# Second product of a fused attention and feed-forward kernel: tokens stationary, or w_out stationary in 64-row tiles

## The chip, the cores and the metric

The kernel runs on one core of a Trainium2 chip. The metric is the device time of one execution in microseconds (us): lower is better. Besides the times there is a profile of one execution, which lists every instruction of the engines with its start and length.

The engines that matter are TensorE (PE: matrix products; its weight loads are listed as PEld), VectorE (DVE: elementwise work, 32x32 block transposes), ScalarE (ACT: activation functions, copies and casts) and SyncE (SP), whose queue issues all DMA transfers of this kernel. SBUF is the on-chip memory of 128 partitions; PSUM holds what TensorE sums, in 8 banks of 128 partitions x 512 fp32 numbers.

## The reference

Two stages in float32 over 32768 tokens of 192 features. The first is a dynamic convolution over 7 tokens with softmax weights of 8 heads; the second a feed-forward network with a squared ReLU.

```python
w = exp(weight_gen - max(weight_gen, -1)); w = w / (sum(w, -1) + 1e-9)
out = einsum('bshk,bskhg->bshg', w, x_unf)   # x_unf: the token and the 6 before it
h = out @ w_in            # 192 -> 2048
r = maximum(h, 0)
g = r * r
y = g @ w_out             # 2048 -> 192
```

The weights of the second stage come in as float64 and are decoded on the chip.

## The kernel before

**Tiles and precision.** 64 chunks of 512 tokens (four tiles of 128) are worked through in order. To keep fp32 precision at the speed of TensorE's reduced format (`F32R`), each operand is split into a high part, a cast to that format (ACT), and a low part, the rest (a subtraction on DVE); a product is the sum of high x high, low x high and high x low.

**First product, `mm1(c, j)`.** It makes two of the 16 feature blocks (128 of the 2048 hidden features x 512 tokens), `fb = 2j` and `2j + 1`. The 192 input features are three pieces of 64 (`k` = 0, 1, 2), so the matmuls contract over 64 rows, and the two blocks use the upper and the lower 64 rows of the array side by side. The order of the 9 pairs is: `xh` pieces 0, 1, 2; `xl` pieces 0, 1, 2; `xh` pieces again with the low weights: 18 matmuls of 512 columns. The results lie in a ring of 4 PSUM banks `ph`.

**Between the products.** For each block ACT takes the ReLU out of PSUM into `rg`, squares it in place and casts it to `gh` (`high`; in every chunk from the third the cast of 6 of the 16 blocks is on DVE instead), and DVE makes `gl = rg - gh` (`low`).

**Second product, `mm2(c, fb)`.** A tile of 128 tokens of `gh` or `gl` is stationary (128 x 128), and the weights stream past it: 384 columns (high and low `w_out`) for `gh`, 192 for `gl`, so four pairs of matmuls for each block, summed over 16 blocks in four PSUM banks `acc0` to `acc3` (one per token tile, one buffer each). The sums lie with tokens on partitions. `finish` copies each bank out with ACT, `store` adds the two halves on DVE and writes 512 tokens to memory. Chunk 0 and half of the blocks of chunk 1 use plain fp32 matmuls.

**Attention.** `conv_steps(c, 0)` gives 20 steps for a chunk: 6 of softmax, 13 multiplications and additions of 128 x 768 on DVE, and a turn: a DVE block transpose to `xr`, four transfers to DRAM (`xd`) and two back (`xT`), so that features lie on partitions. Three `split` steps, one for each piece `k`, then make `xh` (a cast on ACT) and `xl` (a subtraction on DVE), which `mm1` of that chunk reads. Since this turn leaves the tokens in another order, `relu` restores it with a permuted write in all chunks from the third.

**Order.** The schedule is written out by hand (`tc.manual_schedule()`): each engine runs its instructions in program order. A chunk has 32 slots: in the first 16 `mm1` stands in every second slot, in the last 16 `mm2(c, 0)` to `mm2(c, 15)` follow one another; `plan` and `plan_conv` hang everything else on slots. The three splits for the next chunk are on slots 27 to 29 of 32.

Of the kernel before, what the change touches and what calls it, by code (L numbers as in the profile page):

```python
# [19 lines left out]
def kernel(  # L20
# [9 lines left out]
    nc = tc.nc  # L30
    B, S, D = x.shape
# [3 lines left out]
    P = 128  # L35
    Q = 32
# [3 lines left out]
    TC = 4  # L40
    NCH = n_chunks or R // TC
    TG = 8
    CPG = TG // TC
    NF = FF // P
    D1 = 64
    ND = D // D1
    N = TC * P
    NJ = NF // 2
    NU = NJ // 2
    WI = ND * P  # L50
    WC = WI + 2 * D
    NSLOT = 2 * NF
    N_PE = 2
    DVE_CAST = 6
    SQ_EARLY = 7
    X_SLOT = 27
    CONV_BEG = 14
    CONV_END = 12

    const = ctx.enter_context(tc.tile_pool(name="const", bufs=1))  # L60
    stage = ctx.enter_context(tc.tile_pool(name="stage", bufs=3))
    xin = ctx.enter_context(tc.tile_pool(name="xin", bufs=2))
    att = ctx.enter_context(tc.tile_pool(name="att", bufs=1))
    xtp = ctx.enter_context(tc.tile_pool(name="xtp", bufs=1))
    gp = ctx.enter_context(tc.tile_pool(name="gp", bufs=8))
    op = ctx.enter_context(tc.tile_pool(name="op", bufs=1))
    dram = ctx.enter_context(tc.tile_pool(name="dram", bufs=2, space=bass.MemoryType.DRAM))
    ps_h = ctx.enter_context(tc.tile_pool(name="ps_h", bufs=4, space=bass.MemoryType.PSUM))
# [7 lines left out]

    ident = const.tile([P, P], F32, name="ident")
    warm = const.tile([P, 1], F32, name="warm")
    W = const.tile([P, 2, NJ, WC], F32R, name="W")

    ctx.enter_context(tc.manual_schedule())

# [51 lines left out]
    def decode_steps(u):  # L134
        raw = raws.pop(u)
        lo, hi = raw[:, :, :, 0], raw[:, :, :, 1]
        w = stage.tile([P, 2, WI], U32, name="du", bufs=4)
        wf = w.bitcast(F32)
        wfull[u] = wf
        j, c0 = 2 * (u % NU), WI * (u // NU)  # L140
        wh, wl = (W[:, q, j:j + 2, c0:c0 + WI] for q in range(2))
        ts, stt = nc.vector.tensor_scalar, nc.vector.scalar_tensor_tensor
        return [
            lambda: nc.scalar.activation(wf, hi.bitcast(F32), AF.Abs),  # L144
            lambda: ts(out=wf, in0=wf, scalar1=MAG_MIN, scalar2=MAG_MAX, op0=ALU.max, op1=ALU.min),
            lambda: ts(out=w, in0=w, scalar1=3, scalar2=0x3FFFFFFF, op0=ALU.logical_shift_left, op1=ALU.bitwise_and),
            lambda: stt(out=w, in0=hi, scalar=0xC0000000, in1=w, op0=ALU.bitwise_and, op1=ALU.bitwise_or),  # L147
            lambda: stt(out=w, in0=lo, scalar=29, in1=w, op0=ALU.logical_shift_right, op1=ALU.bitwise_or),  # L148
            lambda: nc.scalar.copy(wh, wf),  # L149
            lambda: nc.vector.tensor_tensor(out=wl, in0=wf, in1=wh.bitcast(F32), op=ALU.subtract),  # L150
        ]

    decs = {}
# [129 lines left out]

    def relu(c, fb):
        ph = phs.pop((c, fb))
        r = rgs[c, fb] = gp.tile([P, N], F32, name="rg", bufs=NF)
        if c >= N_PE:
            nc.scalar.activation(  # L288
                r.rearrange("p (t q j) -> p t q j", q=P // Q, j=Q),
                ph.rearrange("p (q t j) -> p t q j", q=P // Q, j=Q),  # L290
                AF.Relu,
            )
        else:
            nc.scalar.activation(r, ph, AF.Relu)  # L294

    def square(c, fb):
        r = rgs[c, fb]
        nc.scalar.activation(r, r, AF.Square)  # L298

    def high(c, fb, on_dve):  # L300
        gh = ghs[c, fb] = gp.tile([P, N], F32R, name="gh")
        (nc.vector.tensor_copy if on_dve else nc.scalar.copy)(gh, rgs[c, fb])  # L302

    def low(c, fb):
        gl = gls[c, fb] = gp.tile([P, N], F32R, name="gl")
        nc.vector.tensor_tensor(out=gl, in0=rgs.pop((c, fb)), in1=ghs[c, fb].bitcast(F32), op=ALU.subtract)  # L306

    def in_fp32(c, fb):
        return c == 0 or c == 1 and 1 <= fb <= NF // 2

    def mm2_tile(c, fb, t):
        acc = accs[c][t]
        j, i = divmod(fb, 2)
        sl = slice(WI + i * D, WI + (i + 1) * D)
        ts_ = slice(t * P, (t + 1) * P)
        first, last = fb == 0, fb == NF - 1
        if in_fp32(c, fb):
            nc.tensor.matmul(acc[:, 0:D], rgs[c, fb][:, ts_], wfull[NU + j // 2][:, j % 2, i * D:(i + 1) * D], start=first, stop=last)  # L318
            return
        wo = W[:, :, j, sl]  # L320
        two = [
            (acc[:, 0:2 * D].rearrange("p (q d) -> p q d", q=2), ghs[c, fb][:, ts_], wo),
            (acc[:, 0:D], gls[c, fb][:, ts_], wo[:, 0, :]),
        ]
        if last:
            two.reverse()
        for n, (o, l, rr) in enumerate(two):
            nc.tensor.matmul(o, l, rr, start=(first and n == 0), stop=(last and n == 1))  # L328

    def mm2(c, fb):  # L330
        if fb == 0:
            accs[c] = [ps_o.tile([P, 512], F32, name=f"acc{t}") for t in range(TC)]
        for t in range(TC):
            mm2_tile(c, fb, t)
        if in_fp32(c, fb):
            del rgs[c, fb]
        else:
            del ghs[c, fb], gls[c, fb]

    outs = {}  # L340
# [86 lines left out]
    slots = {}

    def at(c, s, f):
        slots.setdefault((c + s // NSLOT, s % NSLOT), []).append(f)  # L430

    def spread(fs, c, s0, s1):
        for i, f in enumerate(fs):
            at(c, s0 + (s1 - s0) * i // len(fs), f)

    def plan(c):
        for fb in range(NF):
            at(c, fb - fb % 2, lambda fb=fb: relu(c, fb))
        for t in range(TC):
            at(c, 4 * t + 1, lambda t=t: finish(c - 1, t))  # L440
        at(c, 4 * TC - 2, lambda: store(c - 1, 0, TC))
        for fb in range(NF):
            early = fb < SQ_EARLY
            at(c, 2 * fb + 2 if early else NF + fb - SQ_EARLY, lambda fb=fb: square(c, fb))
            if in_fp32(c, fb):
                continue
            on_dve = fb < DVE_CAST and c > 1
            s = 2 * fb + 3 if on_dve else NF + fb - DVE_CAST
            at(c, s, lambda fb=fb, d=on_dve: high(c, fb, d))
            at(c, s, lambda fb=fb: low(c, fb))  # L450

    def plan_conv(m):
        a, b = conv_steps(m, 0) if m > 2 else (conv2[6:], split2)
        if m > 3:
            spread(a, m - 2, CONV_BEG, NSLOT + CONV_END)
        elif m == 3:
            spread(a, 1, NF + 2, NSLOT + CONV_END)
        else:
            spread(a, 1, 0, NF)
        for k, f in enumerate(b):  # L460
            at(m - 1, X_SLOT + k, f)

    for c in range(1, NCH):
        if c == 1:
            plan_conv(2)
            for u, k in ((2, NF + 2), (3, NF + 4), (1, NF + 7)):
                at(1, k, lambda u=u: dec(NU + u, 6))
        plan(c)
        for s in range(NSLOT):
            if s == 2 and c % 2 and (c + 3) // 2 * CPG < NCH:  # L470
                load_group((c + 3) // 2)
            if s == CONV_BEG - 1 and c + 2 < NCH:
                plan_conv(c + 2)
            if s < NF and s % 2 == 0:
                mm1(c, s // 2)
            if s >= NF and not (c == NCH - 1 and s >= NSLOT - 4):
                mm2(c, s - NF)
            for f in slots.pop((c, s), []):
# [38 lines left out]
```

## Time and profile before

| What | Value |
|---|---|
| Time, median of 3 runs | 2278.14 us (2277.9 to 2278.43) |
| Time of the profiled execution | 2278.05 us |
| Span of the profile (first to last instruction) | 2276.3 us |
| DVE busy | 1903.1 us (84%) |
| ACT busy | 1705.7 us (75%) |
| Granted TensorE clock | 1.000 |
| DMA bytes, mean rate | 158.86 MB, 70 GB/s |

The span is what the profile can explain; 1.75 us of the profiled execution lie outside it. A busy time counts the time in which an engine has at least one instruction under way; matmuls overlap, so PE's own busy time says little about its pace, and the distance between starts is the better measure. In rows of the timeline the columns are start, length, engine, line, operation, `out<-in`, shapes, count of merged instructions, and in brackets the idle time before with what ended it.

### The profile page before, as it was taken

How to read it: one execution, taken by the hardware profiler on the slowest of the kernel's cores; microseconds unless marked ns; L12 is line 12 of the kernel's file. 1: busy time of each engine (PE TensorE's matmuls, PEld its weight loads, DVE VectorE, ACT ScalarE, POOL GpSimd, SP SyncE). 2: the span in 40 equal slices, each digit the busy share in tenths (PEclk: the TensorE clock that was granted, in tenths of full speed). 3: DMA queues.
4: the chain of work that ended last, by engine and by line, in shares of the span. 5: the costliest groups of instructions: out<-in, count | busy, mean ns of one | idle time of the engine just before them, and what ended most of it. 6: DMA issues, size and time to landing. Idle time of an engine off the chain costs nothing.

```text
span 2276.3 us, 45075 instructions
## 1 busy us (share of the span) xinstructions
PE 2259.1 (99%) x17648; PEld 2070.4 (91%) x17648; DVE 1903.1 (84%) x2944; ACT 1705.7 (75%) x3206; POOL 1.7 (0%) x7
## 2 busy tenths in 40 slices
PE   7999999999999999999999999999999999999999
PEld 6898999999989999999899999998998999989988
DVE  8888888888888888888888888888888888888884
ACT  5587787787877877878778778777787787777877
POOL 0000000000000000000000000000000000000000
PEclk9999999999999999999999999999999999999999
DMA  6132221322212312213223133131231221322211
GB/s 168 57 85 64 78 82 32 85 78 64 85 36 78 85 57 85 53 61 85 64 78 84 30 84 85 57 85 36 77 85 59 83 60 54 85 69 73 56 33 39
DMA packets 102134, 158.86 MB, mean 70 GB/s; under 512 B 8488, under 2 KB 65704, under 8 KB 97952
## 3 DMA queue, kind: packets, MB, share of 16 engines
q1 hardware_dynamic: 101920, 155.97, 24.5%
q8 instruction: 138, 2.26, 0.4%
q14 instruction: 76, 0.62, 0.1%
HBM read 106.39 MB, written 49.55 MB: 69 GB/s over the span
## 4 chain that ended last, share of the span: by engine, by line
PE 98%; DVE 1%; DMA 0%; ACT 0%; issue 0%; SPq 0%; DVEq 0%; ACTq 0%
PE acc L328 51%; PE ph L280 46%; PE acc L318 1%; DMA xt<-in_x_dram 0%; PE ph L237 0%; DVE pr L195 0%; DVE pr L200 0%; ACT rg L294 0%; DMA raw<-in_moe_w_in_dram 0%; ACT rg L298 0%; ACT du L144 0%; ACT W L149 0%; DVE du L147 0%; DVE du L148 0%; DVE W L150 0%
## 5 line engine op out<-in xcount | busy, mean ns | idle before, releaser
L328 PE MATMUL acc<-W,gh 128*128 128x384 f32 x4000 | 1153.6, 361 | 0.0
L328 PE MATMUL acc<-W,gl 128*128 128x192 f32 x4000 | 992.1, 251 | 0.0
L288 ACT ACTIVATE rg<-ph 128x512 f32<-128x512 f32 x992 | 539.9, 597 | 507.6 <-PE ph L280 495.5
L306 DVE TENSOR_TENSOR gl<-rg,gh 128x512 fp32r<-128x512 f32 x1000 | 691.0, 691 | 201.3 <-ACT gh L302 158.8
L280 PE MATMUL ph<-xh,W 64*128 64x512 f32 x6144 | 802.0, 389 | 3.1 <-ACT W L149 1.7
L328 PEld LDWEIGHTS acc<-W,gh 128*128 128x128 f32 x4000 | 750.8, 188 | 22.2 <-DVE gl L306 21.2
L328 PEld LDWEIGHTS acc<-W,gl 128*128 128x128 f32 x4000 | 762.7, 191 | 0.0
L280 PEld LDWEIGHTS ph<-xh,W 64*128 64x128 f32 x6144 | 588.1, 184 | 115.9 <-issue 11.6
L298 ACT ACTIVATE rg<-rg 128x512 f32<-128x512 f32 x1024 | 644.4, 631 | 0.0
L280 PE MATMUL ph<-xl,W 64*128 64x512 f32 x3072 | 435.3, 387 | 0.0
L195 DVE TENSOR_TENSOR pr<-xt,wt 128x768 f32<-128x768 f32 x448 | 425.7, 951 | 1.4 <-DMA xt<-in_x_dram 1.4
L302 ACT CAST gh<-rg 128x512 fp32r<-128x512 f32 x628 | 389.1, 620 | 18.0
L200 DVE TENSOR_TENSOR pr<-pr 128x768 f32<-128x768 f32 x381 | 362.4, 951 | 0.4
L280 PEld LDWEIGHTS ph<-xl,W 64*128 64x128 f32 x3072 | 296.7, 184 | 52.8 <-DVE xl L220 0.4
L302 DVE CAST gh<-rg 128x512 fp32r<-128x512 f32 x372 | 155.5, 418 | 149.6 <-ACT rg L298 145.5
L351 ACT COPY raw<-acc 128x384 f32<-128x384 f32 x252 | 121.6, 483 | 4.1 <-PE acc L328 4.1
L220 DVE TENSOR_TENSOR xl<-xT,xh 128x512 fp32r<-128x512 f32 x186 | 122.2, 684 | 0.0
L219 ACT CAST xh<-xT 128x512 fp32r<-128x512 f32 x186 | 102.7, 616 | 0.5 <-DMA xT<-xd 0.5
L357 DVE TENSOR_TENSOR o_sb<-raw 128x768 f32<-128x768 f32 (+1 forms) x64 | 60.1, 939 | 4.7 <-ACT raw L351 4.7
L254 DVE STREAM_TRANSPOSE xr<-pr 128x768 f32<-128x768 f32 x62 | 60.2, 971 | 0.0
L181 ACT ACTIVATE wt<-wt 128x224 f32<-128x224 f32 x64 | 24.0, 376 | 13.7 <-DVE wt L180 13.7
L318 PE MATMUL acc<-du,rg 128*128 128x192 f32 x192 | 31.7, 327 | 0.0
(30 smaller groups left out, 269.3 us busy)
## 6 DMA issues: line engine op xcount, KB each, us to landing
xT<-xd SPq DMA_DIRECT2D x124, 384.0 KB, 5.1
xt<-in_x_dram SPq DMA_DIRECT2D x31, 1344.0 KB, 8.7
out_dram<-o_sb SPq DMA_DIRECT2D x63, 384.0 KB, 5.6
xd<-xr SPq DMA_DIRECT2D x248, 96.0 KB, 2.0
wt<-in_weight_gen_dram SPq DMA_DIRECT2D x31, 224.0 KB, 5.5
raw<-in_moe_w_in_dram SPq DMA_DIRECT2D x16, 192.0 KB, 4.0
raw<-in_moe_w_out_dram SPq DMA_DIRECT2D x4, 768.0 KB, 4.6
xt<-in_x_dram SPq DMA_DIRECT2D x2, 384.0 KB, 4.3
```

The costliest lines, as they stand in the source:

```text
L195: tt(out=dst, in0=src, in1=wk.broadcast_to([P, n, G]), op=ALU.mult)
L200: tt(out=prs[k0], in0=prs[k0], in1=prs.pop(k), op=ALU.add)
L219: nc.scalar.copy(xh, src[k])
L220: tt(out=xl, in0=src[k], in1=xh.bitcast(F32), op=ALU.subtract)
L254: nc.vector.transpose(xr.rearrange("p b (t j) -> p t b j", j=Q), prs.pop(0).rearrange("p t (b i) -> p t b i", i=Q),)
L280: nc.tensor.matmul(two[i], w, xx[rows, k], start=(n == 0), stop=(n == len(seq) - 1))
L288: nc.scalar.activation(r.rearrange("p (t q j) -> p t q j", q=P // Q, j=Q), ph.rearrange("p (q t j) -> p t q j", q=P // Q, j=Q), AF.Relu,)
L298: nc.scalar.activation(r, r, AF.Square)
L302: (nc.vector.tensor_copy if on_dve else nc.scalar.copy)(gh, rgs[c, fb])
L306: nc.vector.tensor_tensor(out=gl, in0=rgs.pop((c, fb)), in1=ghs[c, fb].bitcast(F32), op=ALU.subtract)
L328: nc.tensor.matmul(o, l, rr, start=(first and n == 0), stop=(last and n == 1))
L351: nc.scalar.copy(tmp[:, t, :], acc[:, 0:2 * D])
```

## The change

- **Second product, chunks 1 to 62** (`mm2_turned`): 64 rows x 128 columns of `w_out` are stationary and 64 rows x 512 tokens of `gh` or `gl` stream past, upper and lower half of the array side by side as in `mm1`. For each block there are five pairs: part A (output features 0 to 127) takes high x `gh`, high x `gl`, low x `gh` in banks 0 and 1; part B (64 high columns of features 128 to 191 beside 64 low ones) takes `gh` and `gl` in banks 2 and 3. Chunk 0 (fp32) and chunk 63 keep the old form. `w_out` lies in a tile `V` of its own, with its column order changed.
- **Sums** (`sum_turned`): ACT copies banks 2 and 0 into `X`, DVE adds banks 3 and 1, and one transfer brings the 64 low-part rows of B to partitions 0 to 63.
- **Turning back** (`store_turned`): part 0 is a DVE block transpose of 128 x 512 and 16 transfers of 32 partitions x 4 x 32 numbers into `o_sb`; part 1 is an addition of 64 x 512, a transpose of 64 x 512, 8 such transfers and the store. `relu` needs no permuted write any more, except in chunk 63.
- **Order**: a chunk has 8 steps. In step j, PE runs `mm1(c, j)` and then the two blocks of `mm2_turned` that are two steps older; ACT two ReLUs, two squares, what is planned for the step, then two casts (all 16 casts of a chunk are on ACT); DVE first the two `low`s of the step before (`late`), then what is planned (`todo`), then `store_turned`, then `sum_turned`. The attention of chunk m is spread over steps 4 to 7 of chunk m - 2 and 0 to 3 of chunk m - 1; the splits for chunk m stand in steps 6 (pieces 0 and 1) and 7 (piece 2) of chunk m - 1, ahead of the other planned work. `sum_turned(c)` comes in step 1 of chunk c + 1, `store_turned(c, ·)` in its steps 5 and 6.
- **Buffers**: two for `xh` and `xl` instead of one; 8 each of `rg`, `gh`, `gl` instead of 16, 8, 8.

```diff
+    LAG = 2
+    CONV_BEG = 4
+    OUT_STEP = 5
+    NBUF = NF // 2
...
-    xtp = ctx.enter_context(tc.tile_pool(name="xtp", bufs=1))
-    gp = ctx.enter_context(tc.tile_pool(name="gp", bufs=8))
+    xtp = ctx.enter_context(tc.tile_pool(name="xtp", bufs=2))
+    gp = ctx.enter_context(tc.tile_pool(name="gp", bufs=NBUF))
...
+    def mm2_turned(c, fb):
+        if fb == 0:
+            accs[c] = [ps_o.tile([P, N], F32, name=f"acc{t}") for t in range(4)]
+        gh, gl = ghs.pop((c, fb)), gls.pop((c, fb))
+        j, i = divmod(fb, 2)
+        first, last = fb == 0, fb == NF - 1
+        A, B = [(0, 0, gh), (0, 0, gl), (0, 1, gh)], [(2, None, gh), (2, None, gl)]
+        seq = B + A if last or first else A + B
+        for n, (b, q, g) in enumerate(seq):
+            k = sum(1 for m in seq[:n] if m[0] == b)
+            for h in range(2):
+                rows = slice(h * D1, (h + 1) * D1)
+                w = V[rows, fb, P:2 * P] if q is None else V[rows, fb, 2 * P * q:2 * P * q + P]
+                fl = dict(start=first and k == 0, stop=last and k == (2 if b == 0 else 1))
+                nc.tensor.matmul(accs[c][b + h], w, g[rows], **fl)
+
+    def sum_turned(c):
+        acc = accs[c]
+        X = works[c] = stage.tile([P, 3, N], F32, name="raw")
+        for k, b in ((1, 2), (0, 0)):
+            nc.scalar.copy(X[:, k], acc[b])
+        for k, b in ((1, 2), (0, 0)):
+            nc.vector.tensor_tensor(out=X[:, k], in0=acc[b + 1], in1=X[:, k], op=ALU.add)
+        nc.sync.dma_start(out=X[0:D1, 2], in_=X[D1:P, 1])
+
+    def store_turned(c, part):
+        X = works[c]
+        if part == 0:
+            o_sb = op.tile([P, TC, D], F32, name="o_sb", bufs=2)
+            Y = stage.tile([P, 2, N], F32, name="raw")
+            outs[c] = o_sb, Y
+            nc.vector.transpose(Y[:, 0], X[:, 0])
+        else:
+            nc.vector.tensor_tensor(out=X[0:D1, 1], in0=X[0:D1, 1], in1=X[0:D1, 2], op=ALU.add)
+            nc.vector.transpose(outs[c][1][0:D1, 1], X[0:D1, 1])
...
+        for e in range(P // Q if part == 0 else D1 // Q):
+            d0 = part * P + e * Q
+            for q in range(P // Q):
+                nc.sync.dma_start(
+                    out=o_sb[q * Q:(q + 1) * Q, :, d0:d0 + Q],
+                    in_=y[e * Q:(e + 1) * Q, q],
+                )
+        if part:
+            nc.sync.dma_start(out=out_v[:, c * TC:(c + 1) * TC, :], in_=o_sb)
...
+    def plan_conv(m, a, b):
+        spread(a, max(m - 2, 1), CONV_BEG if m > 2 else 0, CONV_BEG + (NJ if m > 2 else 0))
         for k, f in enumerate(b):
+            at(m - 1, NJ - 2 + k // 2, f)
...
     for c in range(1, NCH):
+        tail = c == NCH - 1
+        for j in range(NJ):
+            if j == 0 and c % 2 and (c + 3) // 2 * CPG < NCH:
                 load_group((c + 3) // 2)
+            if j == CONV_BEG and c + 2 < NCH:
+                plan_conv(c + 2, *conv_steps(c + 2, 0))
...
+            mm1(c, j)
+            fbs = (2 * j, 2 * j + 1)
+            done = None
+            if len(pend) == LAG or tail and pend:
+                c2, j2 = pend.pop(0)
+                for fb in (2 * j2, 2 * j2 + 1):
+                    mm2_turned(c2, fb)
+                done = c2 if j2 == NJ - 1 else None
+            for fb in fbs:
+                relu(c, fb)
+            for fb in fbs:
+                square(c, fb)
+            if not tail:
+                pend.append((c, j))
+            for f in late:
                 f()
+            late.clear()
+            for f in todo.pop((c, j), []):
+                f()
+            if c > 1 and j == OUT_STEP:
+                store_turned(c - 1, 0)
+            if c > 1 and j == OUT_STEP + 1:
+                store_turned(c - 1, 1)
+            if done is not None:
+                sum_turned(done)
+            if not tail or j < NJ // 2:
+                for fb in fbs:
+                    high(c, fb)
+                    late.append(lambda c=c, fb=fb: low(c, fb))
```

More of the change, by code (lines that the diff above doesn't have):

```diff
@@ L50 @@
     WI = ND * P
-    WC = WI + 2 * D
-    NSLOT = 2 * NF
     N_PE = 2
[L54 to L58, printed above, removed]
+    LAG = 2
+    CONV_BEG = 4
+    OUT_STEP = 5
+    NBUF = NF // 2
     const = ctx.enter_context(tc.tile_pool(name="const", bufs=1))
@@ L78 @@
     warm = const.tile([P, 1], F32, name="warm")
-    W = const.tile([P, 2, NJ, WC], F32R, name="W")
+    W = const.tile([P, 2, NJ, WI], F32R, name="W")
+    V = const.tile([P, NF, 2 * D], F32R, name="V")
     ctx.enter_context(tc.manual_schedule())
@@ L139, in decode_steps, with wh, wl @@
         wfull[u] = wf
-        j, c0 = 2 * (u % NU), WI * (u // NU)
-        wh, wl = (W[:, q, j:j + 2, c0:c0 + WI] for q in range(2))
+        if u < NU:
+            to = [[(W[:, q, 2 * u:2 * u + 2, :], slice(None))] for q in range(2)]
+            parts = wf
+        else:
+            f = slice(4 * (u - NU), 4 * (u - NU + 1))
+            to = [[(V[:, f, 0:D], slice(0, D))], [(V[:, f, 2 * P:], slice(0, P)), (V[:, f, D:2 * P], slice(P, D))]]
+            parts = wf.rearrange("p j (f e) -> p (j f) e", f=2)
+        def wh():
+            for o, sl in to[0]:
+                nc.scalar.copy(o, parts[:, :, sl])
+        def wl():
+            for o, sl in to[1]:
+                if u < NU:
+                    h = to[0][0][0]
+                else:
+                    h = V[:, f, sl]
+                nc.vector.tensor_tensor(out=o, in0=parts[:, :, sl], in1=h.bitcast(F32), op=ALU.subtract)
         ts, stt = nc.vector.tensor_scalar, nc.vector.scalar_tensor_tensor
@@ L148, in decode_steps @@
             lambda: stt(out=w, in0=lo, scalar=29, in1=w, op0=ALU.logical_shift_right, op1=ALU.bitwise_or),
-            lambda: nc.scalar.copy(wh, wf),
-            lambda: nc.vector.tensor_tensor(out=wl, in0=wf, in1=wh.bitcast(F32), op=ALU.subtract),
+            wh,
+            wl,
         ]
@@ L285, in relu @@
         ph = phs.pop((c, fb))
-        r = rgs[c, fb] = gp.tile([P, N], F32, name="rg", bufs=NF)
-        if c >= N_PE:
+        if c == 0:
+            r = gp.tile([P, N], F32, name="gh" if fb < NBUF else "gl")
+        else:
+            r = gp.tile([P, N], F32, name="rg")
+        rgs[c, fb] = r
+        if c == NCH - 1:
             nc.scalar.activation(
@@ L298, in square, with high @@
         nc.scalar.activation(r, r, AF.Square)
-    def high(c, fb, on_dve):
+    def high(c, fb):
         gh = ghs[c, fb] = gp.tile([P, N], F32R, name="gh")
-        (nc.vector.tensor_copy if on_dve else nc.scalar.copy)(gh, rgs[c, fb])
+        nc.scalar.copy(gh, rgs[c, fb])
     def low(c, fb):
@@ L306, in low @@
         nc.vector.tensor_tensor(out=gl, in0=rgs.pop((c, fb)), in1=ghs[c, fb].bitcast(F32), op=ALU.subtract)
-    def in_fp32(c, fb):
-        return c == 0 or c == 1 and 1 <= fb <= NF // 2
     def mm2_tile(c, fb, t):
@@ L313, in mm2_tile @@
         j, i = divmod(fb, 2)
-        sl = slice(WI + i * D, WI + (i + 1) * D)
         ts_ = slice(t * P, (t + 1) * P)
         first, last = fb == 0, fb == NF - 1
-        if in_fp32(c, fb):
+        if c == 0:
             nc.tensor.matmul(acc[:, 0:D], rgs[c, fb][:, ts_], wfull[NU + j // 2][:, j % 2, i * D:(i + 1) * D], start=first, stop=last)
             return
-        wo = W[:, :, j, sl]
         two = [
-            (acc[:, 0:2 * D].rearrange("p (q d) -> p q d", q=2), ghs[c, fb][:, ts_], wo),
-            (acc[:, 0:D], gls[c, fb][:, ts_], wo[:, 0, :]),
+            (acc[:, 0:2 * D], ghs[c, fb][:, ts_], V[:, fb]),
+            (acc[:, 0:D], gls[c, fb][:, ts_], V[:, fb, 0:D]),
         ]
@@ L334, in mm2 @@
             mm2_tile(c, fb, t)
-        if in_fp32(c, fb):
+        if c == 0:
             del rgs[c, fb]
@@ L338, in mm2 @@
             del ghs[c, fb], gls[c, fb]
+    def mm2_turned(c, fb):
[13 more added lines that the diff above has]
+                nc.tensor.matmul(accs[c][b + h], w, g[rows], **fl)
+    works = {}
+    def sum_turned(c):
[13 more added lines that the diff above has]
+            nc.vector.transpose(Y[:, 0], X[:, 0])
+        else:
+            nc.vector.tensor_tensor(out=X[0:D1, 1], in0=X[0:D1, 1], in1=X[0:D1, 2], op=ALU.add)
+            nc.vector.transpose(outs[c][1][0:D1, 1], X[0:D1, 1])
+        o_sb, Y = outs[c]
+        y = Y[:, part].rearrange("p (t q i) -> p q t i" if c < N_PE else "p (q t i) -> p q t i", t=TC, i=Q)
+        for e in range(P // Q if part == 0 else D1 // Q):
[7 more added lines that the diff above has]
+            nc.sync.dma_start(out=out_v[:, c * TC:(c + 1) * TC, :], in_=o_sb)
     outs = {}
@@ L356, in store @@
         if c > 0:
-            nc.vector.tensor_tensor(out=o_sb[:, tsl], in0=tmp[:, tsl, 0:D], in1=tmp[:, tsl, D:2 * D], op=ALU.add)
+            for h, l in ((slice(0, P), slice(2 * P, 2 * D)), (slice(P, D), slice(D, 2 * P))):
+                nc.vector.tensor_tensor(out=o_sb[:, tsl, h], in0=tmp[:, tsl, h], in1=tmp[:, tsl, l], op=ALU.add)
         nc.sync.dma_start(out=out_v[:, c * TC + t0:c * TC + t1, :], in_=o_sb[:, tsl])
@@ L424, with at, spread @@
     dec(NU, 6)
[L427 to L432, printed above, removed]
+    todo, pend, late = {}, [], []
+    def at(c, j, f):
+        todo.setdefault((c + j // NJ, j % NJ), []).append(f)
+    def spread(fs, c, j0, j1):
         for i, f in enumerate(fs):
[L434 to L459, printed above, removed]
+            at(c, j0 + (j1 - j0) * i // len(fs), f)
+    def plan_conv(m, a, b):
+        spread(a, max(m - 2, 1), CONV_BEG if m > 2 else 0, CONV_BEG + (NJ if m > 2 else 0))
         for k, f in enumerate(b):
-            at(m - 1, X_SLOT + k, f)
+            at(m - 1, NJ - 2 + k // 2, f)
@@ L463 @@
+    plan_conv(2, conv2[6:], split2)
+    for u in range(1, NU):
+        at(1, 2 * u, lambda u=u: dec(NU + u, 6))
     for c in range(1, NCH):
[L464 to L470, printed above, removed]
-                load_group((c + 3) // 2)
[L472 to L478, printed above, removed]
-                f()
@@ L480 @@
-    c = NCH - 1
+        tail = c == NCH - 1
+        for j in range(NJ):
+            if j == 0 and c % 2 and (c + 3) // 2 * CPG < NCH:
+                load_group((c + 3) // 2)
+            if j == CONV_BEG and c + 2 < NCH:
+                plan_conv(c + 2, *conv_steps(c + 2, 0))
+            if c == 1 and j == 0:
+                for t in range(TC):
+                    finish(0, t)
+                store(0, 0, TC)
+            mm1(c, j)
[13 more added lines that the diff above has]
+            for f in late:
+                f()
+            late.clear()
[11 more added lines that the diff above has]
+                    late.append(lambda c=c, fb=fb: low(c, fb))
@@ L481 @@
+    c = NCH - 1
+    for f in late:
+        f()
+    for fb in range(NF - 4):
+        mm2(c, fb)
+        if fb < NF - NBUF:
+            high(c, fb + NBUF)
+            low(c, fb + NBUF)
     for t in range(TC):
```

## The prediction

> **What bounds the kernel now.** I read the page's chain of work that ended last, then that chain in order of time, then the timeline of each engine over one chunk.
>
> ```profile
> PE 98%; DVE 1%; DMA 0%; ACT 0%; issue 0%; SPq 0%; DVEq 0%; ACTq 0%
> ```
>
> ```profile
> 715.00 18.42 PE acc L328 x128
> 749.97 18.42 PE acc L328 x128
> ...
> 2253.82 18.43 PE acc L328 x128
> ```
>
> ```profile
> 67.22 1.25 PE L280 MATMUL ph<-xh,W 64*128 64x512 f32 x6
> ...
> 701.23 0.85 PE L280 MATMUL ph<-xl,W 64*128 64x512 f32 x6
> ...
> 713.47 0.85 PE L280 MATMUL ph<-xl,W 64*128 64x512 f32 x6
> ...
> 714.15 0.85 PE L280 MATMUL ph<-xh,W 64*128 64x512 f32 x6
> 714.93 0.44 PE L328 MATMUL acc<-W,gh 128*128 128x384 f32 x1
> 715.29 0.36 PE L328 MATMUL acc<-W,gh 128*128 128x384 f32 x1
> ...
> 733.06 0.36 PE L328 MATMUL acc<-W,gh 128*128 128x384 f32 x1
> ```
>
> PE sets the end: 98% of the chain. From 715.00 to 749.97 a chunk takes 34.97 us, 18.42 of it `mm2` and so 16.55 `mm1`. Six `mm1` calls lie between 701.23 and 713.47: 2.04 us each, 0.1133 us for each of 18 matmuls. In `mm2` the second to the last of 64 pairs start 62 distances apart, (733.06 - 715.29) / 62 = 0.287 us each, 18.34 for all. 8 x 2.04 + 18.34 = 34.66; the remaining 0.3 us goes at the two borders between the products.
>
> DVE and ACT have room, but only in total:
>
> ```profile
> 715.00:749.97 34.97, 34.97 (x273) 32.08 (x273) 29.61 (x47) 26.54 (x50) 0.00 (x0) 1.00 0.19 46
> ```
>
> The columns are the stretch, its length, then PE, PEld, DVE and ACT busy, POOL, clock, DMA share, GB/s.
>
> **PE after the change.** A chunk's second product becomes 16 blocks x 5 pairs x 2 = 160 matmuls of 64x512, the form of `mm1`; at 0.1133 us that is 18.13 us. With `mm1` at 16.32 the floor is 34.45 us, 0.52 below now. Bounds: at `mm1`'s rate with its borders (16.55 / 144 = 0.115) the gain is nothing. I take 0.1133, since `mm1`'s own group borders cost nothing in the rows above. [...]
>
> From 67.22, where `mm1(1, 0)` starts, the last matmul now ends 2205.0 us later (2253.82 + 18.43). After: 63 x 16.32 + 62 x 18.13 + 18.42 = 2170.7. That is 34.3 us less, before any wait.
>
> **What ACT and DVE do in a step** decides whether PE gets there.
>
> ```profile
> 749.12 0.85 PE L280 MATMUL ph<-xh,W 64*128 64x512 f32 x6
> ```
>
> ```profile
> 735.72 1.09 ACT L288 ACTIVATE rg<-ph 128x512 f32<-128x512 f32 x2 [6.06 <-PE ph L280]
> ...
> 750.00 1.09 ACT L288 ACTIVATE rg<-ph 128x512 f32<-128x512 f32 x2
> 750.97 0.63 ACT L298 ACTIVATE rg<-rg 128x512 f32<-128x512 f32 x1
> 751.64 0.62 ACT L302 CAST gh<-rg 128x512 fp32r<-128x512 f32 x1
> 752.16 0.63 ACT L298 ACTIVATE rg<-rg 128x512 f32<-128x512 f32 x1
> ...
> 762.97 1.66 ACT L219 CAST xh<-xT 128x512 fp32r<-128x512 f32 x3
> ```
>
> ```profile
> 726.37 0.95 DVE L195 TENSOR_TENSOR pr<-xt,wt 128x768 f32<-128x768 f32 x1
> 727.23 0.69 DVE L306 TENSOR_TENSOR gl<-rg,gh 128x512 fp32r<-128x512 f32 x1
> 727.84 0.95 DVE L195 TENSOR_TENSOR pr<-xt,wt 128x768 f32<-128x768 f32 x1
> ...
> 736.33 0.95 DVE L195 TENSOR_TENSOR pr<-xt,wt 128x768 f32<-128x768 f32 x1
> 739.40 0.43 DVE L302 CAST gh<-rg 128x512 fp32r<-128x512 f32 x1 [2.12 <-ACT rg L298]
> ...
> 740.54 0.95 DVE L200 TENSOR_TENSOR pr<-pr 128x768 f32<-128x768 f32 x1
> ...
> 751.61 0.38 DVE L179 TENSOR_REDUCE mx<-wt 128x32 f32<-128x224 f32 x1
> 752.02 0.39 DVE L180 TENSOR_TENSOR wt<-wt,mx 128x224 f32<-128x224 f32 x1
> ```
>
> Read from these: six matmuls take 0.68 to issue and 0.85 to end, and the ReLU follows 0.03 later, so it starts 0.2 us after PE passes to the next work. The squares start 0.97 after the first ReLU; independent ACT operations follow at 0.52 to 0.53 (751.64 to 752.16; (1.66 - 0.62) / 2). On DVE, 128x768 takes 0.87 to the next start and 128x512 0.61; a dependent operation starts 0.04 after its forerunner's end (751.61 + 0.38 to 752.02). DVE works strictly in order: at 737.28 to 739.40 it sits 2.12 us on a cast's wait, and the ready addition behind it runs at 740.54.
>
> A step of PE is 2.04 + 2 x 1.133 = 4.31 us. ACT's six operations need 3.1 to 3.2 of it, eight of them 4.2: hidden behind PE, although all casts are ACT's now. On DVE per chunk the change removes 6 casts at 0.43 and the 0.95 addition of `store`, 3.5 us, and adds two PSUM additions, an addition and two transposes:
>
> ```profile
> L288 ACT ACTIVATE rg<-ph 128x512 f32<-128x512 f32 x992 | 539.9, 597 | 507.6 <-PE ph L280 495.5
> ...
> L220 DVE TENSOR_TENSOR xl<-xT,xh 128x512 fp32r<-128x512 f32 x186 | 122.2, 684 | 0.0
> L254 DVE STREAM_TRANSPOSE xr<-pr 128x768 f32<-128x768 f32 x62 | 60.2, 971 | 0.0
> L184 DVE TENSOR_TENSOR wt<-wt,sm 128x224 f32<-128x224 f32 x64 | 24.6, 385 | 0.1
> ...
> L294 ACT ACTIVATE rg<-ph 128x512 f32<-128x512 f32 x32 | 17.5, 604 | 8.1 <-PE ph L280 8.1
> ...
> L220 DVE TENSOR_TENSOR xl<-ph,xh 128x512 fp32r<-128x512 f32 x6 | 4.0, 686 | 0.4 <-ACT xh L219 0.4
> ```
>
> From PSUM 0.69, from SBUF 0.69, a transpose of 512 columns about 0.7 (0.97 less a third of its size): 3.5 again. So the total stays near 29.6; what changes is the order. (The ReLU's permuted write, 597 ns at L288 against 604 plain at L294, costs nothing now and saves nothing.)
>
> **The wait it adds.** Follow step 6 of a chunk, time 0 being when PE goes from `mm1(c, 6)` to the second product. ReLUs from 0.20, squares from 1.17 and 1.70, `xh` piece 0 at 2.23 to 2.85, piece 1 to 3.38. DVE finished the `low`s early (their casts ended 0.9 us before 0) and waits with `xl` 0 until 2.88. Behind it in its queue: `xl` 1 (from 3.48), the softmax multiplication (4.1 to 4.5), two attention multiplications (from 4.5 and 5.4), the addition (6.2) and transpose (7.0) of `store_turned` part 1, step 7's two `low`s (7.6, 8.2), and only then `xl` 2, at 8.8 to 9.5. PE meanwhile runs `mm2` 2.27, `mm1(c, 7)` 2.04, `mm2` 2.27 and ten matmuls of `mm1(c + 1, 0)`, 1.13, and at 7.7 needs `xl` 2 for its eleventh. The wait is per slice, as in chunk 0:
>
> ```profile
> 21.14 0.98 PE L280 MATMUL ph<-xh,W 64*128 64x512 f32 x6 [1.07 <-ACT W L149]
> ...
> 21.60 0.69 DVE L220 TENSOR_TENSOR xl<-ph,xh 128x512 fp32r<-128x512 f32 x1 [0.18 <-ACT xh L219]
> ```
>
> There `mm1` began at 21.14, before the last `xl` piece was made. So PE stands still for 9.5 - 7.7 = **1.8 us at each border of chunks**. The two 64-partition operations have no row; if they cost nothing the wait is 0.55, if each costs a 128x768 operation it is 2.3. I take 1.8, from the rows of equal column count. Borders from chunk 2 to 61 all have this queue: 60 x 1.8 = 108 us. At 62 no attention is left to make, and the wait is about 0.2 (`xh` 2).
>
> Later waits: with PE delayed, DVE enters the next chunk 0.7 us into step 0, is 0.2 late in step 1, and ends its last bank addition 4.5 into it; `mm2(c + 1, 0)` reaches that bank at 4.3 + 0.45. That holds by 0.25 us. The turn ends at 2.7 in step 3; SP then needs
>
> ```profile
> 748.46 1.79 SPq L260 DMA_DIRECT2D xd<-xr  x4
> 753.61 1.24 SPq L265 DMA_DIRECT2D xT<-xd  x2
> ...
> xT<-xd SPq DMA_DIRECT2D x124, 384.0 KB, 5.1
> ```
>
> 753.61 - 748.46 = 5.2 to the second issue and 1.2 + 5.1 to landing, 14.2 after step 3 began at the latest; `xh` 0 asks at 12.9 + 2.2 = 15.1. The 24 small transfers at 1.79 / 4 = 0.45 us hold SP for 11 us from step 5 on, and the store behind them waits for their landing. Next in its queue are the loads of step 0, `sum_turned`'s transfer of step 1 and `xd` of step 3, which alone is urgent, some 15 us later: hidden.
>
> **One-time terms.** In chunk 1's first four steps DVE has 14 attention operations (12.2 us), eight `low`s and two weight subtractions, 19 us against some 13 of PE: I put 6 us. In the last chunk ACT holds up the six `mm1`s that stand alone: 24 to 28 operations at 0.53 against 12.2 us of PE, about 1.5.
>
> **Sum**, against the profiled execution: 2276.3 - 34.3 + 108 + 0.2 + 6 + 1.5 = 2357.7 of span; with the 1.75 outside, **2359 us** (the median of the runs stands 0.1 above that execution).
>
> **Rivals.**
> - *No queue at the border (faster).* If `xl` 2 came within 0.45 us of PE's need, the 26.7 us left of the floor would win. At zero the time is 2251. The deciding point is DVE's queue between `xl` 0 and `xl` 2, 5.9 us long: it must shrink by 1.35, about the addition and transpose together. For it: they have no row. Against: same column counts elsewhere. 11%; within 0.2% another 4%.
> - *The margin of 0.25 us at the bank goes.* If DVE is 1 us later in step 1, `mm2(c + 1, 0)` waits too, as does the chain after it: up to 1 us x 60, 2420. 15%.
> - *Small transfers.* They are 24 x 128 = 3072 packets of 128 B a chunk, 192 for each of 16 engines. Part 0 can start at 1.7 in step 5 and all must land by step 3 of the next chunk, some 27 us: at above 0.14 us a packet SP's queue holds `xd` back, `xT` comes late, and each chunk grows to the transfers' own length; at 0.21 that is 40 us, 2277 + 62 x 5 = 2587.
>
> ```profile
> 748.40:753.60 5.20, 5.20 (x40) 4.68 (x39) 4.43 (x10) 5.07 (x11) 0.00 (x0) 1.00 0.38 79
> ```
>
> 0.38 x 5.2 x 16 / 768 `xd` packets of 512 B is 0.04 us each: far off. [...] 4%.
> - *Alternating costs 0.15 us each time*: 16 x 0.15 = 2.4 a chunk, less 0.45 of the wait (three of them lie before it): 2359 + 62 x 1.95 = 2480. 4%.
>
> **How the numbers follow.** Forecast 62%. Its own range goes with the wait from 0.55 to 2.3: 2284 to 2390. The range 2273 to 2430 also takes in the case of no change and the bank's wait, 81% together; outside lie the faster case and the last two. A measurement of this kernel tells 0.2% (4.6 us) from no change; faster 0.11, same 0.04, slower 0.85.
>
> **What would show it.** Right: chunk period 36.2 us; PE before L280 idle about 1.8 us a chunk, released by DVE `xl`; DVE idle about 3 us before `xl`, released by ACT `xh`; no idle time at other steps; 160 matmuls in 18.1 us. Wrong: PE waiting on ACT, on `acc` or not at all; a matmul distance in the second product above 0.115; `xT` landing after step 6.

## The result and the profile after

The changed kernel takes 2367.39 us (median of 4 runs, 2366.52 to 2367.76) against 2278.02 us of the kernel before on the same chip: 1.0392 times as long, 95% interval 1.0374 to 1.041. The prediction was 2359 us. The profiled execution took 2366.52 us, its span is 2364.7 us.

PE no longer sets the end alone. The page's chain of work that ended last, after:

```profile
PE 70%; DVE 16%; ACT 7%; issue 4%; SPq 1%; DMA 1%; DVEq 0%; ACTq 0%
PE ph L296 34%; PE acc L370 34%; DVE pr L211 5%; DVE xl L236 5%; ACT rg L314 3%; DVE gl L326 3%; ACT rg L318 2%; DVE raw L391 2%; SPq L398 1%; ACT xh L235 1%; PE acc L334 1%; DVE wt L200 1%; PE acc L343 1%; DMA o_sb<-raw 1%; DVE pr L216 0%
```

Where PE had 98% before, the chain now runs at every border of chunks through ACT (ReLU L314, square L318, `xh` L235) and DVE (`xl` L236, the attention's L211, part 1 of the turning back, L391, `low` L326). That list is the queue that the prediction spelled out. (The 2% of SPq and DMA come from nine borders at which the profile puts DVE's wait for the first `xh` down to a landing of `o_sb`; it is 3.0 us there too, as long as where it is put down to ACT's cast.) PE's timeline shows the place (start, length, engine, line, operation, shapes, count, idle time before and its releaser):

```profile
1006.21 0.84 PE L296 MATMUL ph<-xh,W 64*128 64x512 f32 x6
...
1010.51 1.11 PE L296 MATMUL ph<-xh,W 64*128 64x512 f32 x6
1011.46 0.63 PE L296 MATMUL ph<-xl,W 64*128 64x512 f32 x4
1013.42 0.50 PE L296 MATMUL ph<-xl,W 64*128 64x512 f32 x2 [1.33 <-DVE xl L236]
1013.75 0.86 PE L296 MATMUL ph<-xh,W 64*128 64x512 f32 x6
1014.45 0.40 PE L370 MATMUL acc<-gh,V 64*128 64x512 f32 x2
...
1050.82 0.39 PE L370 MATMUL acc<-gh,V 64*128 64x512 f32 x2
```

A step is 1010.51 - 1006.21 = 4.30 us. The `mm1` at the border begins at 1010.51 and the next work at 1014.45: 3.94 us instead of 2.04, so the border costs 1.90. 0.27 of it stands in the first row (1.11 for six matmuls instead of 0.84: `xh` piece 2), 1.51 before the eleventh matmul (1013.42 - 1011.46 for four matmuls that need 0.45), and 0.12 in the eight matmuls behind it. A chunk is 1050.82 - 1014.45 = 36.37 us. DVE in the same stretch:

```profile
1002.49 1.29 DVE L326 TENSOR_TENSOR gl<-rg,gh 128x512 fp32r<-128x512 f32 x2 [1.26 <-ACT gh L322]
1006.80 1.29 DVE L236 TENSOR_TENSOR xl<-xT,xh 128x512 fp32r<-128x512 f32 x2 [3.01 <-ACT xh L235]
1008.01 0.39 DVE L200 TENSOR_TENSOR wt<-wt,sm 128x224 f32<-128x224 f32 x1
1008.43 1.83 DVE L211 TENSOR_TENSOR pr<-xt,wt 128x768 f32<-128x768 f32 x2
1010.17 0.68 DVE L391 TENSOR_TENSOR raw<-raw 64x512 f32<-64x512 f32 x1
1010.88 0.70 DVE L392 STREAM_TRANSPOSE raw<-raw 64x512 f32<-64x512 f32 x1
1011.52 1.24 DVE L326 TENSOR_TENSOR gl<-rg,gh 128x512 fp32r<-128x512 f32 x2
1012.69 0.68 DVE L236 TENSOR_TENSOR xl<-xT,xh 128x512 fp32r<-128x512 f32 x1
```

DVE sits 3.01 us on the first cast of `xh`, and while PE goes on it then works through everything in front of `xl` piece 2, which ends at 1013.37; PE starts 0.05 later. The views of waits over the whole run give the same in sum:

```profile
DVE xl L236 <- ACT xh L235: 159.8, 56, 3.0
PEld ph L296 <- DVE xl L236: 108.4, 64, 1.8
PE ph L296 <- DVE xl L236: 81.0, 61, 1.3
```

Columns: total us, times, longest. 60 waits of PE of 1.33 us, and one of 1.19 at the border from chunk 1 to 2, are 81 us. The profile counts idle time only from the modelled end of the last matmul; by distances between starts each of the 60 borders costs 1.90, and these 114 us turned a floor below the old time into a loss of 89.

### The profile page after: what moved, and what is told of

Same layout as the page of the kernel before. It is cut to its first block, busy times and chain, and to the rows that moved or that the text cites. A ratio compares the mean times of both kernels' runs of the same rounds, so it can differ in the third digit from the quotient of the medians.

```text
span 2364.7 us, 50238 instructions
## 1 busy us (share of the span) xinstructions
PE 2264.6 (96%) x19632; PEld 1846.5 (78%) x19632; DVE 1871.6 (79%) x2834; ACT 1799.4 (76%) x3462; POOL 1.7 (0%) x7
## 4 chain that ended last, share of the span: by engine, by line
PE 70%; DVE 16%; ACT 7%; issue 4%; SPq 1%; DMA 1%; DVEq 0%; ACTq 0%
PE ph L296 34%; PE acc L370 34%; DVE pr L211 5%; DVE xl L236 5%; ACT rg L314 3%; DVE gl L326 3%; ACT rg L318 2%; DVE raw L391 2%; SPq L398 1%; ACT xh L235 1%; PE acc L334 1%; DVE wt L200 1%; PE acc L343 1%; DMA o_sb<-raw 1%; DVE pr L216 0%
## 5 line engine op out<-in xcount | busy, mean ns | idle before, releaser
L370 PE MATMUL acc<-gh,V 64*128 64x512 f32 x5952 | 1010.3, 386 | 0.0
L314 ACT ACTIVATE rg<-ph 128x512 f32<-128x512 f32 x992 | 539.0, 596 | 512.6 <-PE ph L296 505.4
L296 PE MATMUL ph<-xh,W 64*128 64x512 f32 x6144 | 882.9, 389 | 5.2 <-ACT xh L235 2.2
L326 DVE TENSOR_TENSOR gl<-rg,gh 128x512 fp32r<-128x512 f32 x1008 | 645.4, 679 | 269.2 <-ACT gh L322 269.2
L370 PE MATMUL acc<-gl,V 64*128 64x512 f32 x3968 | 774.9, 386 | 0.3 <-DVE gl L326 0.3
L370 PEld LDWEIGHTS acc<-gh,V 64*128 64x128 f32 x5952 | 560.8, 184 | 115.2
L318 ACT ACTIVATE rg<-rg 128x512 f32<-128x512 f32 x1008 | 581.2, 633 | 0.0
L322 ACT CAST gh<-rg 128x512 fp32r<-128x512 f32 x1008 | 577.0, 628 | 2.6 <-PE acc L343 2.6
L370 PEld LDWEIGHTS acc<-gl,V 64*128 64x128 f32 x3968 | 373.8, 184 | 77.3 <-DVE gl L326 0.7
L211 DVE TENSOR_TENSOR pr<-xt,wt 128x768 f32<-128x768 f32 x448 | 418.9, 947 | 3.1 <-DMA xt<-in_x_dram 0.9
L236 DVE TENSOR_TENSOR xl<-xT,xh 128x512 fp32r<-128x512 f32 x186 | 122.2, 685 | 186.5 <-ACT xh L235 159.4
L235 ACT CAST xh<-xT 128x512 fp32r<-128x512 f32 x186 | 108.8, 621 | 0.4 <-DMA xT<-xd 0.4
L380 DVE TENSOR_TENSOR raw<-acc,raw 128x512 f32<-128x512 f32 x124 | 79.0, 675 | 4.3 <-ACT raw L378 4.3
L378 ACT COPY raw<-acc 128x512 f32<-128x512 f32 x124 | 66.6, 597 | 0.0
L391 DVE TENSOR_TENSOR raw<-raw 64x512 f32<-64x512 f32 x62 | 41.9, 676 | 0.0
```

Of the source, the lines that this page charges most:

```text
L211: tt(out=dst, in0=src, in1=wk.broadcast_to([P, n, G]), op=ALU.mult)
L235: nc.scalar.copy(xh, src[k])
L236: tt(out=xl, in0=src[k], in1=xh.bitcast(F32), op=ALU.subtract)
L296: nc.tensor.matmul(two[i], w, xx[rows, k], start=(n == 0), stop=(n == len(seq) - 1))
L322: nc.scalar.copy(gh, rgs[c, fb])
L370: nc.tensor.matmul(accs[c][b + h], w, g[rows], **fl)
```

## The experiments

Theory: the new form of the product is faster on PE; the loss is a matter of order on DVE, whose queue holds `xl` piece 2 behind work that nobody waits for. Rivals: ACT's casts are the true bound; the form or the alternation is slow in itself; the small transfers hold something back.

**All three splits in step 6, ahead of the attention operations.**

```diff
-            at(m - 1, NJ - 2 + k // 2, f)
+            at(m - 1, NJ - 2, f)
```

> The third split (xh and xl piece 2) moves from step 7 to step 6, right behind the other two and ahead of the attention operations. Theory (DVE's order as a whole): the wait of 1.9 us at the border of chunks goes, but DVE's work is only pushed back by it. Counted with the changed kernel's own starts, DVE ends the bank additions of step 1 at 18.5 and 19.1 us after step 6's second product began, and PE wants the banks at 17.2: a new wait of about 1.45 us before the second product's first block, released by the bank additions. Chunk 35.95 us, time about 2342. Rival 1 (the border wait is all there is to win): chunk 34.47, time about 2253. Rival 2 (ACT's casts are what PE waits for, DVE only comes last by chance): as the casts of piece 2 move too, about 2253 as well, and the extra DVE operation of the next run would cost nothing. Rival 3 (the new form or the alternation itself is slower): no change, 2367.

Measured: 2334.66 us (ratio to the kernel before 1.025, interval 1.0234 to 1.0265). PE's timeline over this stretch has one wait a chunk, and it is the one that was computed:

```profile
1008.67 0.49 PE L370 MATMUL acc<-gh,V 64*128 64x512 f32 x1 [0.79 <-DVE raw L380]
1044.53 0.50 PE L370 MATMUL acc<-gh,V 64*128 64x512 f32 x1 [0.76 <-DVE raw L380]
```

PE waits for `raw` of L380, the additions that empty the PSUM banks; the weight load ahead of the same work waits too (91.1 us in 122 waits in that run's view of waits). A chunk is 35.86 us, 0.1 below the expectation. Of the 1.9 us won at the border 1.4 came back as a new wait, because DVE had lost its 3 us in step 6 all the same and had only been pushed back. A border that is all there is to win, ACT's casts as what PE waits for (2253 both), and the form or the alternation as cause (2367) are out.

**One DVE operation more, in step 6 or in step 5.** The transpose of part 1, or of part 0, is issued twice:

```diff
             nc.vector.transpose(outs[c][1][0:D1, 1], X[0:D1, 1])
+            nc.vector.transpose(outs[c][1][0:D1, 1], X[0:D1, 1])
```

> One DVE operation more in step 6: the transpose of 64x512 in part 1 of the turning back is done twice (0.64 us to the next start). Theory: it stands in the queue ahead of xl piece 2, and PE waits for each of the 60 borders that much longer: 2367 + 38 = 2405. Rival 2 (ACT's casts set the wait) and rival 3 (the form or the alternation): 2367, within 3.

> The same dose one step earlier: the transpose of 128x512 in part 0 is done twice (0.6 us). Theory: DVE idles 1.3 us behind it, waiting for a cast, so it costs nothing: 2367, within 3. If DVE's total work set the time, it would cost as much as in step 6, about 2404.

Measured: step 5, 2367.86 us: nothing, as expected, since the operation falls into an idle time. Step 6, 2438.65 us: 71 us more, not 38. So the place decides, as the theory has it, and ACT's casts, which this edit does not touch, are not what PE waits for; but the size was missed, for two reasons. The first is the dose. From DVE's timeline of that run:

```profile
1040.02 0.70 DVE L392 STREAM_TRANSPOSE raw<-raw 64x512 f32<-64x512 f32 x1
1040.76 0.70 DVE L393 STREAM_TRANSPOSE raw<-raw 64x512 f32<-64x512 f32 x1
1041.39 1.24 DVE L326 TENSOR_TENSOR gl<-rg,gh 128x512 fp32r<-128x512 f32 x2
```

The second transpose starts 0.74 us after the first, 0.04 behind its end, where the `low` of another tile starts 0.63 after a transpose. The second is the clock. The run's stretches (PE, PEld, DVE, ACT and POOL busy, then the granted clock, DMA share, GB/s) show it:

```profile
1040.60:1043.30 2.70, 0.63 (x8) 0.19 (x4) 2.67 (x6) 0.65 (x2) 0.00 (x0) 1.00 0.12 18
1043.30:1048.20 4.90, 4.90 (x29) 4.03 (x31) 4.90 (x7) 2.81 (x6) 0.00 (x0) 0.65 0.17 29
```

PE idles 2.07 us in the first row. In the second its clock is granted at 0.65 on average (0.50 for 3.41 us of it), with 29 matmuls in 4.9 us where 43 fit at 0.1133. This does not happen at each border, as the expectation of the next run has it: the trace's record of the granted clock has such a fall behind 18 of the 60. Over the run a chunk takes 37.10 us at a border without a fall, 0.74 more than in the changed kernel, and 38.59 at one with a fall: 60 x 0.74 + 18 x 1.49 = 71 us.

**Half that dose** (a transpose of 64x256).

> The changed kernel with half the dose in step 6: a transpose of 64x256 more (about 0.37 us to the next start). The full dose cost 71 us, not 38; its trace shows a granted clock of 0.65 for about 5 us behind each border wait, which grew to 2.07 us of idle PE. If the clock falls in proportion to the wait: 2367 + 41 = 2408. If it falls only past a length of wait between 1.33 and 2.07: 2367 + 22 = 2389, or that and the full 33 us more, 2422.

Measured: 2438.38 us, as much as the full dose. None of the three figures came out. Again the second transpose starts 0.74 us after the first, so half the dose is 0.47 and not 0.37, and PE's wait at each border is 1.33 + 0.47 = 1.80 us; but the clock falls behind some borders and not behind others. From PE's timeline, two borders in a row:

```profile
1004.70 0.50 PE L296 MATMUL ph<-xl,W 64*128 64x512 f32 x2 [1.80 <-DVE xl L236]
1005.03 0.86 PE L296 MATMUL ph<-xh,W 64*128 64x512 f32 x6
...
1041.53 0.56 PE L296 MATMUL ph<-xl,W 64*128 64x512 f32 x2 [1.79 <-DVE xl L236]
1041.88 1.49 PE L296 MATMUL ph<-xh,W 64*128 64x512 f32 x6
```

After the first the six matmuls take 0.86, after the second, with the same wait, 1.49. The clock falls behind 26 of the 60 borders. A chunk takes 36.85 us without a fall (0.49 more than in the changed kernel) and 38.43 with one: 60 x 0.49 + 26 x 1.58 = 70 of the 71 measured. So the dose acts as the queue says, and the rest is the clock. Why it falls behind one wait and not behind an equal one is taken up in the last section.

**The splits in step 6, behind the attention operations.** On DVE these then fill the 3 us before the first cast of `xh`.

```diff
-            at(m - 1, NJ - 2 + k // 2, f)
+            last_in.setdefault((m - 1, NJ - 2), []).append(f)
...
             for f in todo.pop((c, j), []):
                 f()
+            for f in last_in.pop((c, j), []):
+                f()
```

> All three splits in step 6, but behind the attention operations of that step (on DVE), so that the softmax multiplication and the two attention multiplications, 2.2 us, fill the 3 us in which DVE waits for the first cast. Theory: xl piece 2 is ready some 3 us before PE asks for it, and DVE enters the next chunk as early as now relative to PE, so no wait takes the place of the old one: chunk 34.47 us, time 2367 - 61 x 1.9 = about 2252, faster than the kernel before by 1.1%. Rival 1 of the first run gives the same. If the bank additions still come late (DVE short of time in total), between 2252 and 2342.

Measured: 2247.42 us, ratio 0.9867 (0.985 to 0.9883): faster than the changed kernel, and 1.3% below the kernel before, clear of the noise. DVE's timeline has the same operations as above in another order:

```profile
1021.10 1.29 DVE L326 TENSOR_TENSOR gl<-rg,gh 128x512 fp32r<-128x512 f32 x2 [1.26 <-ACT gh L322]
1022.31 0.39 DVE L200 TENSOR_TENSOR wt<-wt,sm 128x224 f32<-128x224 f32 x1
1022.73 1.83 DVE L211 TENSOR_TENSOR pr<-xt,wt 128x768 f32<-128x768 f32 x2
1025.41 1.90 DVE L236 TENSOR_TENSOR xl<-xT,xh 128x512 fp32r<-128x512 f32 x3 [0.85 <-ACT xh L235]
1027.22 0.68 DVE L391 TENSOR_TENSOR raw<-raw 64x512 f32<-64x512 f32 x1
```

The idle time of 3.01 is 0.85, all of `xl` is done at 1027.3, and no matmul of the stretch has idle time before it. PE's timeline, the same product one chunk apart, and a stretch of about a chunk:

```profile
1020.50 1.06 PE L296 MATMUL ph<-xh,W 64*128 64x512 f32 x6
...
1054.96 1.06 PE L296 MATMUL ph<-xh,W 64*128 64x512 f32 x6
```

```profile
1000.00:1034.47 34.47, 34.47 (x308) 28.51 (x306) 29.11 (x46) 27.92 (x55) 0.00 (x0) 1.00 0.27 62
```

A chunk is 1054.96 - 1020.50 = 34.46 us, the floor. DVE's 29.11 us of work are the same as in the changed kernel (29.02 in 36.37). The order alone is worth 120 us.

**Small transfers replaced, on that version.**

```diff
-        for e in range(P // Q if part == 0 else D1 // Q):
-            d0 = part * P + e * Q
-            for q in range(P // Q):
-                nc.sync.dma_start(
-                    out=o_sb[q * Q:(q + 1) * Q, :, d0:d0 + Q],
-                    in_=y[e * Q:(e + 1) * Q, q],
-                )
+        of = o_sb.rearrange("p t d -> p (t d)")
+        if part == 0:
+            nc.sync.dma_start(out=of[:, 0:N], in_=Y[:, 0])
+        else:
+            nc.sync.dma_start(out=of[0:D1, N:], in_=Y[0:D1, 1, 0:N // 2])
+            nc.sync.dma_start(out=of[D1:, N:], in_=Y[0:D1, 1, N // 2:])
```

> On the version with the splits in step 6 behind the attention operations: the 24 small transfers of a chunk are replaced by three with runs of 1 and 2 KB that carry the same bytes without the turn of blocks (the output is then in another order). Theory: the small transfers are hidden behind PE, so the time stays at 2247, within 4. Rival: if SP's queue or the transfer engines held anything back, the time falls by what they cost.

Measured: 2247.88 us, no change. 1488 transfers of 16 KB are hidden.

**The old form in the new order**, on the same version: `mm2` in the place of `mm2_turned`, `finish` and `store` in the place of `sum_turned` and `store_turned`, the permuted ReLU from chunk 2.

```diff
-                    mm2_turned(c2, fb)
+                    mm2(c2, fb)
```

> On the same version: the second product keeps its old form (tokens stationary, 128 rows, sums with tokens on partitions, copied and added as before), but stands in the new order, alternating with the first product 16 times a chunk. If a change of the array's tiling costs 0.15 us each time, as read from the two borders of the kernel before: chunk 16.32 + 18.34 + 16 x 0.15 = 37.1 us, time about 2247 + 61 x 2.6 = 2406. If alternating itself is free: chunk 34.7, time about 2260. In both cases the new form, not the order, is what makes alternating cheap or gives the gain.

Measured: 2456.7 us (ratio 1.0786, 1.077 to 1.0802), above the higher figure. PE's timeline over a step:

```profile
1003.73 0.97 PE L296 MATMUL ph<-xh,W 64*128 64x512 f32 x6
1004.53 0.85 PE L296 MATMUL ph<-xl,W 64*128 64x512 f32 x6
1005.22 0.84 PE L296 MATMUL ph<-xh,W 64*128 64x512 f32 x6
1006.00 0.44 PE L343 MATMUL acc<-V,gh 128*128 128x384 f32 x1
1006.27 0.25 PE L343 MATMUL acc<-V,gl 128*128 128x192 f32 x1
1006.36 0.36 PE L343 MATMUL acc<-V,gh 128*128 128x384 f32 x1
...
1008.45 0.97 PE L296 MATMUL ph<-xh,W 64*128 64x512 f32 x6
```

A step is 1008.45 - 1003.73 = 4.72 us; `mm1` is 2.04 and eight pairs at 0.285 are 2.28, so 0.40 goes at the two changes between 64-row and 128-row work, 0.20 each (0.15 was taken). No matmul of the step has idle time before it. (The profile puts 0.16 us before the first weight load of `mm1` down to ACT's square; in the changed kernel the same `mm1` starts at 1006.21, before that square's end at 1006.26, so it does not need it.) In the new form the same alternation costs nothing (4.30 a step).

**The new form in the old order**: the kernel before with `mm2_turned`, the sums on slot 3 and the turning back on slots 17 and 21 of 32.

```diff
-                mm2(c, s - NF)
+                (mm2 if c == NCH - 1 else mm2_turned)(c, s - NF)
...
+            at(c, 3, lambda: sum_turned(c - 1))
+            at(c, NF + 1, lambda: store_turned(c - 1, 0))
+            at(c, NF + 5, lambda: store_turned(c - 1, 1))
```

> The second product in the new form (64 rows, w_out stationary, turning back) in the order of the kernel before: 16 slots with the first product, then 16 blocks of the second, splits on slots 27 to 29, sums taken on slot 3, turned back on slots 17 and 21. Theory: the form alone gives the gain on PE (34.47 us a chunk, about 2250), and the order of the changed kernel alone caused the loss; DVE has 2.5 us more to do than in the new order (six casts), so some wait is possible, up to 2278. Rival (the new form is slow in itself): above 2278.

Measured: 2249.22 us, ratio 0.9874 (0.9857 to 0.989). Its chain that ended last has PE alone again, with 18.13 us for the 160 matmuls of a second product:

```profile
395.79 18.13 PE acc L367 x160
430.24 18.13 PE acc L367 x160
```

Their distance, 34.45 us, is the predicted floor. So the form (with the tile `V` and without fp32 matmuls in chunk 1, as in the changed kernel) is worth 29 us, and the alternation neither gains nor costs.

## Why the prediction was right, and by how much it missed

- **PE's floor**: 34.45 us a chunk was predicted; 34.46 and 34.45 were measured in the two versions without waits. 0.1133 us a matmul holds for the new form. The sum has no term for changing between the products 16 times a chunk, and no row of the kernel before shows that this is free; a step of 4.30 us in the changed kernel, against 2.04 + 2.27 of work, does.
- **The queue at the border**: from the start of step 6's second product (1003.94), the first `xl` was put at 2.88 and came at 2.86, `xl` piece 2 at 8.8 and came at 8.75, PE's restart at 9.5 and came at 9.48. The two 64-partition operations without a row took 0.68 and 0.70 us, as their column count said.
- **The term that was off**: the border was put at 1.8 and costs 1.90, so a chunk is 36.37 instead of 36.25 us, and 60 x 0.12 = 7 of the 8 us between prediction and result. The wait itself was right: PE's need at 7.70, its restart at 9.48. The eight matmuls behind it take 14.45 - 13.42 = 1.03 us instead of 8 x 0.1133 = 0.91; these 0.12 us behind the restart the sum had left out.
- **The bank's margin**: put at 0.25 us, it held, and was wider. From DVE's and PE's timelines:

```profile
1021.78 1.27 DVE L380 TENSOR_TENSOR raw<-acc,raw 128x512 f32<-128x512 f32 x2
```

```profile
1023.07 0.39 PE L370 MATMUL acc<-gh,V 64*128 64x512 f32 x2
```

The additions end at 1023.05; PE begins the next sums at 1023.07 with part B, whose bank was free 0.6 earlier, and reaches the last bank 0.45 later, so 0.47 us were left. That the margin breaks when only the border is mended, the first experiment showed.
- **Transfers**: SP's issues are slower than thought, 24 in 16.3 us (0.68 each, not 0.45):

```profile
1001.25 16.32 SPq L398 DMA_DIRECT2D o_sb<-raw  x24
...
1029.97 1.85 SPq L276 DMA_DIRECT2D xd<-xr  x4
```

They end 12.4 us before `xd` is issued, and replacing them changed nothing; the equal times show that their cost is hidden, not that it is small. What a packet costs is in the trace of the version with the splits in step 6 behind the attention operations: 12 ns for one of 128 B (median of 190464), 40 ns for one of 512 B, far below the 140 ns at which the rival began.
- **One-time terms**: about 6.7 us were lost from the start of chunk 1's first product to `mm1(2, 1)` (66.81 to 107.72, 40.9 us, against 9 x 2.04 + 7 x 2.266 = 34.2 of work) and 6 was predicted, but not at this place, so that it fits is in part luck. Chunk 1 itself, in whose first four steps the prediction put the 6, lost 1.1 us (66.81 to 97.82, against 29.9 of work). The other 5.6 were lost at the border from chunk 1 to 2 (97.82 to 107.72, 9.9 us against 4.3 of work), for which the prediction has no wait:

```profile
100.67 0.50 PE L296 MATMUL ph<-xh,W 64*128 64x512 f32 x2 [2.24 <-ACT xh L235]
...
102.83 0.62 PE L296 MATMUL ph<-xl,W 64*128 64x512 f32 x2 [1.19 <-DVE xl L236]
```

Behind these two waits the clock was granted at 0.50 from 103.06 to 106.47. ACT, late here, had waited 4.68 us for a softmax operation of DVE at 89.02, so DVE's backlog may have come to PE by way of ACT; that was not tested. The six `mm1`s that stand alone in the last chunk lost 1.55 us (2328.44 to 2342.24, against 12.24 of work), as predicted.
- **The rivals** each failed on their own mark: no wait on `acc`, a step of 4.30, no late `xT`. A price of alternating was measured where the form of the tile changes (0.20 us a change in the old form in the new order), and none in the new form (4.30 a step).

## What to carry to other kernels

A total of busy time says whether an engine can keep up, not whether it does (DVE, busy 29.02 of 36.37 us, held PE up all the same): write out the queue between a late input (here `xh` from ACT) and the operation that the bound engine waits for, and price each entry. In an engine that works in order, as DVE does here (3.01 us idle on the first cast of `xh`, with ready work behind it), put work that is ready ahead of an operation that must wait, not behind it; moving only the late operation forward shifted the wait to the next thing that the engine owed (1.4 of 1.9 us came back). When a product's form and its order change together, try each alone: here the form was worth 29 us, and the order around one step decided 120.

## What the runs showed that was not expected

A wait of PE can cost more than its length, and equal waits can cost differently. With 1.33 us of idle PE the clock fell behind none of the 60 borders; with 1.80 us (half a dose) it fell behind 26, with 2.07 (the full dose) behind 18. It is not the length of the wait alone that decides.

The traces' records of the granted clock show what else does. Each fall behind a border is to 0.50 and lasts 3.41 us, and two falls in a row start 75.09, 112.64 or 150.19 us apart, which is 22, 33 or 44 times 3.413. The waits ahead of them keep the kernel's own distances (75.29 us from 288.58 to 363.87 in the half-dose run, where the falls start at 290.90 and 365.99). So the falls begin on a fixed grid with steps of 3.41 us, which does not follow the kernel. Three steps of this grid around the second of the two borders of the half dose above:

```profile
1038.42:1041.83 3.41, 1.62 (x12) 0.79 (x10) 3.34 (x7) 1.32 (x3) 0.00 (x0) 1.00 0.16 24
1041.83:1045.24 3.41, 3.41 (x18) 2.67 (x16) 3.41 (x6) 1.84 (x4) 0.00 (x0) 0.50 0.14 23
1045.24:1048.65 3.41, 3.41 (x32) 3.11 (x30) 3.41 (x6) 1.31 (x3) 0.00 (x0) 1.00 0.28 89
```

The wait of 1.79 us (1039.74 to 1041.53) lies whole in the first step, and the clock falls in the next. At the border before it the wait (1002.90 to 1004.70) is cut by the grid at 1004.28, so at most 1.38 us lie in one step, and there is no fall. This sorts all 120 borders of the two runs: behind the 44 with a fall at least 1.665 us of idle PE lay within one step, behind the 76 without at most 1.657. A wait of 1.33 us is shorter than that by itself; the two waits at the border from chunk 1 to 2 got there together (1.02 and 1.19 us in the step from 99.65 to 103.06). How many borders are hit depends on how the chunk's length meets the grid, which is why the shorter wait could lose more.

No experiment moved the grid or the waits against it on purpose: what sorts the borders is read from the records of these two runs, and whether it holds elsewhere was not shown.
